# The end of batch 1: where a unit's products and the copies of batch 2's k and q stand

## The chip, the cores and the metric

The kernel runs on one core of one Trainium2 chip. The metric is the device time of one execution in microseconds (us), the median over several runs. A profiled execution gives the trace that the views are taken from. The engines are PE (matrix products; PEld is its loading of weights), DVE (vector), ACT (scalar and activation), POOL (general) and SP (here only a queue that issues DMAs).

## The reference

An attention with a sliding window and a bias by distance, followed by a feed-forward layer with a hard-swish gate:

```
scores = q k^T / sqrt(64) - slope[h] * |i - j|,   kept where 0 <= i - j < 128, else -1e9
attn   = softmax(scores);   x = attn v          # 8 batches, 8 heads, 576 tokens, head size 64
h      = x w_in                                 # 4608 tokens x 512 -> 2048
out    = (h * clip(h + 3, 0, 6) / 6) w_out      # -> 4608 x 512
```

All inputs and the output are float32; the kernel computes its products in bfloat16.

## The kernel before

**Groups.** Attention works on groups of two heads of one batch: `g = 4 * batch + pair`, 32 groups in all; NP is 4. Batch 1 is groups 4 to 7, batch 2 groups 8 to 11. A group's steps are: k and q turned so that the head dimension lies on the partitions (by PE transposes and copies out of PSUM for batches 0 to 2 and k of batch 3, by DMA transposes, line 218, later on); scores (L399 from batch 2 on); exponentials on ACT and cuts by POOL; `attend` or `values`, the products with v (L455, L463) and DVE's division by the row sums (L484, L485); and `back`, which turns the result into `xT`, the input of the feed-forward layer (L517 on PE, the copy L519 on ACT, and on DVE for the last group of batches 0 and 1; by DMA, L510, for most groups from 8 on).

**Units.** The feed-forward layer is cut into token tiles of 512 (`nt`, 9 of them). A tile has 16 up steps (`moe_up`: four 128x512 products over the four pairs of heads, L532; ACT's L556; DVE's L557, which writes `gbuf`) and 16 down steps (`moe_down`, four products L587 each; every fourth ends with a copy and an output DMA). `units` lists them in a fixed order, first the 16 up steps of tile 0 (called unit 0 to 15 here), then up steps of tile 1 (units 16, 17, ...) mixed with down steps of tile 0 by ORDER. `fill(n)` emits the next n of them. `up_begin(nt, ms, n)` emits the first n products of an up step early; the later `fill` completes it. Tile 1 needs all four groups of batch 1 in `xT`, and its fourth product reads the rows of group 7.

**PSUM.** Eight banks: two score tiles of two banks each, used in turn by scores, `attend` and the wide transposes of k and q; "av" and "o" with one buffer each; "h" with two buffers, used in turn. An up step takes a buffer of "h" unless UP_BANKS names another bank for it. A buffer is taken again only when its last reader is done, for an up step DVE's L557. Down steps take "o".

**The order is written by hand.** Each engine runs its instructions in the order of the calls; waits on semaphores are put in for data and buffers. The end of batch 1 is the tail of `second_batch`, lines 773 to 791: attends and backs of groups 4 to 7, the wide transposes of batch 2's first k and q (two pairs of heads in one tile, L301, copies L306), and the last up steps of tile 0. Then follow the first two up steps of tile 1 (the second `fill(2)`), the scores of group 8, and `segment`, which runs groups 8 to 31.

**Loads.** SP's queue issues q, k and v of later batches in order, and also the outputs and the DMA transposes; POOL's queue issues the weights (L176, L190). v of batch 2 starts behind a POOL write at line 768.

Of the kernel before, what the change touches and what calls it, by code (L numbers as in the profile page):

```python
# [18 lines left out]
def kernel(  # L19
# [16 lines left out]
    NP = H // 2  # L36
# [7 lines left out]
    n_ks = d_model // 128  # L44
# [42 lines left out]
    def score_banks():  # L87
        turns[0] += 1
        return score[turns[0] % 2]
# [99 lines left out]
    def load_w_out(g):  # L189
        nc.gpsimd.dma_start(  # L190
            out=w_out_sb[:, ts(g, 4), :],
            in_=moe_w_out[ds(g * 512, 512), :].rearrange("(m p) d -> p m d", p=128))
# [98 lines left out]
    def wide_double(b, dp, nm, copy):  # L291
        wide_begin(b, dp, nm)
        wide_copy(b, dp, nm, 0, 2, copy)

    def wide_begin(b, dp, nm):
        src = st[b, dp, nm]
        wide = score_banks()
        tp = wide.rearrange("p s c -> p (s c)").bitcast(BF16)[:, 0:RT * 128].rearrange(
            "p (t c) -> p t c", t=RT)
        for t in range(RT):  # L300
            nc.tensor.transpose(tp[:, t, :], src[:, t, :], ident)  # L301
        st[b, dp, nm, "wide"] = tp

    def wide_copy(b, dp, nm, i, n, copy):
        dst = (qTb if nm == "q" else kTb)[b % 2][:, ds(2 * dp + i, n), :, :]
        copy(out=dst.rearrange("p i j c -> p i (j c)")[:, :, 0:S].rearrange(  # L306
                 "p i (a t) -> p i a t", t=RT),
             in_=st[b, dp, nm, "wide"].rearrange("p t (a i) -> p i a t", i=2)[:, ds(i, n)])
# [26 lines left out]
    def scores_diag(g):  # L335
        rooms(g)
        b, hp = divmod(g, NP)
        qT, kT = qTb[b % 2][:, hp, :, :], kTb[b % 2][:, hp, :, :]
        first = not diag_tabled(g)
        if (g, "scd") not in st:  # L340
            tables_diag(g)
        scd = st[g, "scd"]
        for j in range(4):
            for e in range(2):
                r = slice(e * D, (e + 1) * D)
                nc.tensor.matmul(scd[:, e, ts(j, 128)], lhsT=kT[r, j, :],
                                 rhs=qT[r, j, :], start=first, stop=first or j == 3)
# [60 lines left out]
    def exp_off_full(g):  # L408
        nc.scalar.activation(out=st[g, "po"].rearrange("p e j c -> p e (j c)"),  # L409
                             in_=st[g, "sco"], func=ACT.Exp, scale=scale)  # L410
# [35 lines left out]
    def av_matmuls(g, qts, where):  # L446
        b, hp = divmod(g, NP)
        vb = vbuf[b % 2]
        pd, po, p4 = st[g, "pd"], st[g, "po"], p4buf[g % 2]
        for qt in qts:  # L450
            for e in range(2):
                h = 2 * hp + e
                out_av = where(qt, e)
                if qt > 0:
                    nc.tensor.matmul(out_av, lhsT=po[:, e, (qt if full(g) else qt - 1) % 4, :],  # L455
                                     rhs=vb[:, qt - 1, h, :], start=True, stop=False)
                if qt < 4:
                    d = pd[:, e, qt, :]
                elif full(g):
                    d = po.rearrange("p e j c -> p e (j c)")[:, e, 64:192]  # L460
                else:
                    d = p4[:, e, :]
                nc.tensor.matmul(out_av, lhsT=d, rhs=vb[:, qt, h, :],  # L463
                                 start=(qt == 0), stop=True)
# [13 lines left out]
    def attend(g):  # L478
        wide = score_banks()
        av = wide[:, :, 0:NQ * W].rearrange("p e (j c) -> p e j c", j=NQ)  # L480
        av_matmuls(g, range(NQ), lambda qt, e: av[:, e, qt, :])
        avs = st[g, "avs"] = small.tile([128, NQ, 2, D], BF16, tag="avs", name="avs")
        rc = small.tile([128, 2, NQ, 1], FP32, tag="rcw", name="rcw")
        nc.vector.reciprocal(rc, av[:, :, :, D:W])  # L484
        nc.vector.tensor_tensor(out=avs.rearrange("p j e d -> p e j d"), in0=av[:, :, :, 0:D],  # L485
                                in1=rc.to_broadcast([128, 2, NQ, D]), op=ALU.mult)
# [16 lines left out]
    def by_xbar(g):  # L503
        return g >= XB and g not in (XB + 2, XB + 3)

    def back(g, tag=None):
        b, hp = divmod(g, NP)
        avs = st[g, "avs"].rearrange("p j e d -> p j (e d)")
        if by_xbar(g):
            nc.sync.dma_start_transpose(  # L510
                out=xT[:, hp, ds(b % 4 * S, SP)].rearrange("p (j c) -> p j c", j=NQ),
                in_=avs.rearrange("p j c -> p (j c)"))
            return
        tag = tag or ("o" if b < 2 else "h")
        tp = BANKS[tag].tile([128, SP], BF16, tag=tag, name="tb", padded_shape=[128, 1024])
        for j in range(NQ):
            nc.tensor.transpose(tp[:, ts(j, 128)], avs[:, j, :], ident)  # L517
        eng = nc.vector.tensor_copy if g in (NP - 1, 2 * NP - 1) else nc.scalar.copy
        eng(out=xT[:, hp, ds(b % 4 * S, S)], in_=tp[:, 0:S])  # L519
# [5 lines left out]
    def up_mms(nt, ms, k0, k1, hps):  # L525
        at0 = nt * NT % RING
        n = min(NT, RING - at0)
        for lo, hi, src in ((0, n, at0), (n, NT, 0)):
            if lo == hi:
                continue  # L530
            for ks in range(k0, k1):
                nc.tensor.matmul(hps[:, lo:hi], lhsT=w_in_sb[:, ks, ts(ms, 128)],  # L532
                                 rhs=xT[:, ks, ds(src, hi - lo)],
                                 start=(ks == 0), stop=(ks == n_ks - 1))

    def up_begin(nt, ms, n, tag="h"):
        hps = BANKS[tag].tile([128, NT], FP32, tag=tag, name="hps")
        up_mms(nt, ms, 0, n, hps)
        begun[nt, ms] = hps, n
# [3 lines left out]
        up_mms(nt, ms, k0, n, hps)  # L543
        begun[nt, ms] = hps, n

    UP_BANKS = {6: "o", 8: "av", 11: "o", 12: "av"}

    def moe_up(nt, ms):
        gts[nt] = gbuf[nt % 2]
        hps, n = begun.pop((nt, ms), (None, 0))  # L550
        if hps is None:
            tag = UP_BANKS.get(ms, "h") if nt == 0 else "h"
            hps = BANKS[tag].tile([128, NT], FP32, tag=tag, name="hps")
# [55 lines left out]
    def fill(n):  # L609
        for _ in range(n):  # L610
            if at[0] == len(units):
                return
            nt, fn, step = units[at[0]]
            if fn is moe_up and done[0] < NP * (min((nt * NT + NT - 1) // S, B - 1) + 1):
                return
            fn(nt if fn is moe_up else nt - 1, step)
            at[0] += 1

    V, P, A = nc.vector.tensor_copy, nc.gpsimd.tensor_copy, nc.scalar.copy
# [109 lines left out]
    def second_batch():  # L729
        scores_diag(NP + 0)  # L730
        exp_diag(NP + 0, 0)
        exp_diag(NP + 0, 1)
        up_begin(0, 2, n_ks, "av")
        scores_off(NP + 0)
        exp_off_full(NP + 0)
        wide_double(1, 1, "k", V)
        fill(2)
        scores_diag(NP + 1)
        exp_diag(NP + 1, 0)
        exp_diag(NP + 1, 1)  # L740
        double(1, 1, "q", 0, "o", V)
        scores_off(NP + 1)
        exp_off_full(NP + 1)
        double(1, 1, "q", 1, "av", V)
        fill(5)
        cast_tokens(1, "v")
        scores_diag(NP + 2)
        exp_diag(NP + 2, 0)
        exp_diag(NP + 2, 1)
        fill(1)  # L750
        scores_off(NP + 2)
        exp_off_full(NP + 2)
        fill(2)
        load_w_out(0)
        load_w_out(1)
        g = 2 * NP - 1
        scores(g)
        exp_diag(g, 0)
        exp_diag(g, 1)
        exp_off_full(g)  # L760
        up_begin(0, 12, n_ks, "av")
        attend(NP)
        fill(1)
        prepare_double(2, 0, (A, P))
        load_w_out(2)
        load_w_out(3)
        prepare_double(2, 1, (P, P))
        nc.gpsimd.memset(ldbuf[2][:, 0:1], 0.0)
        load_tokens(2, "v")
        for dp in range(2):  # L770
            load_double(3, dp, "k", nc.sync)
        load_tokens(3, "q")
        up_begin(0, 13, n_ks)
        attend(NP + 1)
        back(NP, "o")
        attend(NP + 2)
        back(NP + 1, "av")
        attend(NP + 3)
        fill(1)
        back(NP + 2, "o")  # L780
        wide_begin(2, 0, "k")
        wide_copy(2, 0, "k", 0, 2, A)
        up_begin(0, 14, 2)
        back(2 * NP - 1, "av")
        wide_begin(2, 0, "q")
        wide_copy(2, 0, "q", 0, 1, V)
        wide_copy(2, 0, "q", 1, 1, A)
        fill(2)
        done[0] = 2 * NP
        fill(2)  # L790
        scores(2 * NP)
# [98 lines left out]
```

## Time and profile before

| what | value |
|---|---|
| median of 3 runs | 321.89 us (321.74 to 322.06) |
| the profiled execution's own time | 321.99 us |
| its span, first to last instruction | 320.3 us |
| granted PE clock, mean | 0.998 |
| PE busy in 40 to 60 us | 17.55 of 20 us |
| PE busy in 60 to 80 us | 19.82 of 20 us |
| PE busy in 100 to 160 us | 60.00 of 60 us |
| 128x512 product on PE (L532), own duration | 0.38 us; four in a row take 1.03 us |
| L556 on ACT, L557 on DVE | 0.69 us each |

Products overlap on PE, so a row of n lasts less than n times one. A wait is written behind the instruction that waited, with what ended it. An engine's idle time matters only where the end of the run hangs on it.

### The profile page before, as it was taken

Reading aid. Unit: us, or ns where it says so; the run is one execution under the profiler, and the core shown is the slowest. Engines: PE = TensorE matmul, PEld = TensorE weight load, DVE = VectorE, ACT = ScalarE, POOL = GpSimd, SP = SyncE. Lnnn points to the kernel's source line nnn. Section 1 sums busy time; section 2 is a strip of 40 time slices with the busy share of each in tenths; the row PEclk is TensorE's granted clock in tenths of the full one; section 3 lists DMA queues with packets and bytes.
Section 4 is the critical chain, followed back from the end, with each engine's and each line's share of the span. In section 5 each row is a group of like instructions: output and inputs, shape, how many; then the busy total and the mean of one; then the engine's idle time right before and its main releaser. Section 6 shows DMA issues by size and latency. Waiting matters only on the chain.

```text
span 320.3 us, 7022 instructions
## 1 busy us (share of the span) xinstructions
PE 310.0 (97%) x2710; PEld 162.8 (51%) x2710; DVE 175.9 (55%) x344; ACT 197.6 (62%) x339; POOL 138.6 (43%) x247
## 2 busy tenths in 40 slices
PE   7889997999999999999999999999999999999996
PEld 3465463455555444444667654444444444444443
DVE  6677674554445664656455646564656455455510
ACT  3879985777677775767576757675764344244401
POOL 7367290666395685638563855472331000000000
PEclk9999999999999999999999999999999999999999
DMA  7999999889999999999999989925022200100112
GB/s 268 260 371 213 268 239 212 228 208 193 201 255 167 221 226 221 211 221 207 185 177 227 222 183 199 232 60 89 20 55 70 72 33 33 35 33 33 65 53 80
DMA packets 131425, 52.43 MB, mean 164 GB/s; under 512 B 118976, under 2 KB 122816, under 8 KB 131392
## 3 DMA queue, kind: packets, MB, share of 16 engines
q1 hardware_dynamic: 125648, 46.15, 65.7%
q0 software_dynamic: 3696, 3.67, 7.1%
q10 hardware_dynamic: 2048, 2.16, 2.2%
q8 instruction: 21, 0.34, 0.5%
q14 instruction: 12, 0.10, 0.1%
HBM read 36.70 MB, written 9.44 MB: 144 GB/s over the span
## 4 chain that ended last, share of the span: by engine, by line
PE 86%; DMA 5%; ACT 4%; DVE 2%; POOL 1%; issue 1%; SPq 0%; DVEq 0%; POOLq 0%; ACTq 0%
PE ops L587 37%; PE hps L532 37%; PE score L399 3%; DMA ldbuf<-in_q_dram 3%; PE av L463 2%; DMA ldbuf<-in_k_dram 2%; PE av L455 2%; ACT r L556 2%; PE ops L568 1%; DVE gbuf L557 1%; ACT gbuf L425 1%; PE tp L269 1%; PE score L301 1%; ACT gbuf L409 1%; PE tb L517 1%
## 5 line engine op out<-in xcount | busy, mean ns | idle before, releaser
L556 ACT ACTIVATE r<-hps,bias 128x512 f32<-128x512 f32 x144 | 99.0, 689 | 85.3 <-PE hps L532 85.0
L557 DVE SCALAR_TENSOR_TENSOR gbuf<-r,hps 128x512 bf16<-128x512 f32 x144 | 98.7, 687 | 94.3 <-ACT r L556 92.4
L532 PE MATMUL hps<-xT,w_in_sb 128*128 128x512 bf16 (+1 forms) x640 | 143.6, 358 | 2.1 <-DVE gbuf L557 1.8
L587 PE MATMUL ops<-w_out_sb,gbuf 128*128 128x512 bf16 x560 | 138.2, 379 | 0.0
L532 PEld LDWEIGHTS <-w_in_sb 128*128 128x128 bf16 x640 | 59.1, 98 | 55.8 <-issue 3.2
L587 PEld LDWEIGHTS <-gbuf 128*128 128x128 bf16 x560 | 52.4, 98 | 57.5
L427 POOL TENSOR_SCALAR_AFFINE_SELECT pd<-pd 128x512 bf16<-128x512 bf16 x48 | 29.4, 631 | 41.1 <-ACT pd L425 41.1
L436 POOL TENSOR_SCALAR_AFFINE_SELECT po<-po 128x512 bf16<-128x512 bf16 x48 | 30.2, 632 | 32.3 <-ACT po L434 31.6
L596 DVE COPY osb<-ops 128x512 f32<-128x512 f32 x33 | 22.7, 687 | 23.8 <-PE ops L587 23.7
L425 ACT ACTIVATE pd<-score,bias_d 128x512 bf16<-128x512 f32 x48 | 31.1, 684 | 6.4 <-PE score L399 6.4
L434 ACT ACTIVATE po<-score,bias_o 128x512 bf16<-128x512 f32 x48 | 33.1, 690 | 0.0
L213 POOL CAST tbuf<-ldbuf 128x512 bf16<-128x512 f32 (+1 forms) x45 | 25.5, 611 | 12.5 <-issue 12.5
L474 DVE TENSOR_TENSOR avs<-av,rc 128x384 bf16<-128x384 f32 (+1 forms) x48 | 23.6, 491 | 1.6
L463 PEld LDWEIGHTS <-pd 128*128 128x128 bf16 x192 | 14.3, 97 | 8.2 <-POOL tbuf L213 0.2
L455 PE MATMUL av<-vbuf,po 128*128 128x65 bf16 x192 | 18.0, 193 | 0.0
L463 PE MATMUL av<-vbuf,pd 128*128 128x65 bf16 x192 | 17.3, 194 | 0.0
L206 POOL CAST vbuf<-ldbuf 128x1024 bf16<-128x1024 f32 x14 | 14.2, 1041 | 6.0 <-DMA ldbuf<-in_v_dram 6.0
L455 PEld LDWEIGHTS <-po 128*128 128x128 bf16 x192 | 14.3, 98 | 3.0 <-DVE avs L474 0.5
L439 ACT ACTIVATE p4buf<-score,bias_d 128x64 bf16<-128x64 f32 x48 | 15.6, 325 | 0.0
L399 PEld LDWEIGHTS <-kTb 64*64 64x64 bf16 x480 | 9.4, 106 | 9.1 <-issue 8.5
L399 PE MATMUL score<-qTb,kTb 64*64 64x192 bf16 (+1 forms) x480 | 13.1, 234 | 0.0
L246 POOL CAST pr<-ldbuf 128x576 bf16<-128x576 f32 x18 | 11.5, 668 | 2.9 <-ACT w_out_sb L422 1.5
(107 smaller groups left out, 200.7 us busy)
## 6 DMA issues: line engine op xcount, KB each, us to landing
out_dram<-osb SPq DMA_DIRECT2D x33, 256.0 KB, 3.1
ldbuf<-in_v_dram SPq DMA_DIRECT2D x31, 256.0 KB, 4.5
ldbuf<-in_q_dram SPq DMA_DIRECT2D x20, 256.0 KB, 4.6
ldbuf<-in_k_dram SPq DMA_DIRECT2D x16, 256.0 KB, 5.3
ldbuf<-in_q_dram SPq DMA_DIRECT2D x12, 288.0 KB, 6.2
ldbuf<-in_k_dram SPq DMA_DIRECT2D x12, 288.0 KB, 6.1
w_out_sb<-in_moe_w_out_dram POOLq DMA_DIRECT2D x4, 512.0 KB, 9.8
w_in_sb<-in_moe_w_in_dram POOLq DMA_DIRECT2D x3, 512.0 KB, 9.4
```

Of the source, the lines that this page charges most:

```text
L213: nc.gpsimd.tensor_copy(out=tbuf[:m, :, j, :], in_=s[:m, j, :, :].rearrange("p (i e) d -> p i (e d)", e=2))
L399: nc.tensor.matmul(wide[e][c, ds(at, n)], lhsT=kT[r, j, c], rhs=qT[r, ds(q0, n)], start=True, stop=True)
L425: nc.scalar.activation(out=pd[:, e, :, :], in_=block_scores(g, e, False), func=ACT.Exp, bias=bias_d[:, h:h + 1], scale=scale)
L427: nc.gpsimd.affine_select(out=pd[:, e, :, :], in_=pd[:, e, :, :], pattern=[[0, 4], [1, 128]], channel_multiplier=-1, base=0, compare_op=AL ...
L434: nc.scalar.activation(out=po[:, e, :, :], in_=sc, func=ACT.Exp, bias=bias_o[:, h:h + 1], scale=scale)
L436: nc.gpsimd.affine_select(out=po[:, e, :, :], in_=po[:, e, :, :], pattern=[[0, 4], [-1, 128]], channel_multiplier=1, base=-1, compare_op=A ...
L455: nc.tensor.matmul(out_av, lhsT=po[:, e, (qt if full(g) else qt - 1) % 4, :], rhs=vb[:, qt - 1, h, :], start=True, stop=False)
L463: nc.tensor.matmul(out_av, lhsT=d, rhs=vb[:, qt, h, :], start=(qt == 0), stop=True)
L532: nc.tensor.matmul(hps[:, lo:hi], lhsT=w_in_sb[:, ks, ts(ms, 128)], rhs=xT[:, ks, ds(src, hi - lo)], start=(ks == 0), stop=(ks == n_ks - 1))
L556: nc.scalar.activation(out=r6, in_=hps, func=ACT.Relu, bias=bias3[:, 0:1], scale=1.0 / 6.0)
L557: nc.vector.scalar_tensor_tensor(out=gts[nt][:, ms, :], in0=r6, scalar=1.0, in1=hps, op0=ALU.min, op1=ALU.mult)
L587: nc.tensor.matmul(ops[nt, sub], lhsT=gts[nt][:, ms, ts(sub, 128)], rhs=w_out_sb[:, ms, :], start=(ms == 0), stop=(ms == n_ms - 1))
```

## The change

Four things are edited, all around the end of batch 1. Unit 14's products are emitted at once, and ahead of the second back (group 5) rather than in two parts around the last back. The L556 and L557 of units 13 and 14 are emitted together after the last attend, ahead of the copy of group 6's back and of the copies of k and q. The copy of q is one instruction on DVE instead of one half on DVE and one on ACT; k's copy stays one instruction on ACT. Unit 15 takes bank "o" instead of a buffer of "h", so units 16 and 17 take the two "h" buffers that units 13 and 14 held.

```diff
-    UP_BANKS = {6: "o", 8: "av", 11: "o", 12: "av"}
+    UP_BANKS = {6: "o", 8: "av", 11: "o", 12: "av", 15: "o"}
...
         attend(NP + 2)
+        up_begin(0, 14, n_ks)
         back(NP + 1, "av")
         attend(NP + 3)
+        fill(2)
+        back(NP + 2, "o")
+        wide_double(2, 0, "k", A)
+        back(2 * NP - 1, "av")
+        wide_double(2, 0, "q", V)
         fill(1)
-        back(NP + 2, "o")
-        wide_begin(2, 0, "k")
-        wide_copy(2, 0, "k", 0, 2, A)
-        up_begin(0, 14, 2)
-        back(2 * NP - 1, "av")
-        wide_begin(2, 0, "q")
-        wide_copy(2, 0, "q", 0, 1, V)
-        wide_copy(2, 0, "q", 1, 1, A)
-        fill(2)
         done[0] = 2 * NP
         fill(2)
         scores(2 * NP)
```

`wide_double(b, dp, nm, copy)` is `wide_begin` followed by one `wide_copy` of both pairs. Nothing is computed differently.

## The prediction

> **What bounds the kernel now.** The page comes first: its head gives the span of the profiled execution, its first part the busy time of each engine.
>
> ```profile
> span 320.3 us, 7022 instructions
> PE 310.0 (97%) x2710; PEld 162.8 (51%) x2710; DVE 175.9 (55%) x344; ACT 197.6 (62%) x339; POOL 138.6 (43%) x247
> ```
>
> PE is busy for 310.0 of 320.3 us, so a microsecond is to be had only where PE stands still. After the first 28 us, PE's list of waits has two long entries, both in the stretch that the diff edits: 0.58 us ended by DVE's L485 and 1.60 us ended by DVE's L557. From 52 us on there are five waits of 0.08 to 0.18 us and none longer. The table by windows (length, busy time of PE, PEld, DVE, ACT, POOL, granted clock, DMA share, GB/s) shows the place:
>
> ```profile
> 46.00:48.00 2.00, 2.00 (x22) 1.24 (x20) 1.96 (x4) 1.42 (x2) 2.00 (x5) 1.00 1.07 150
> 48.00:50.00 2.00, 0.60 (x3) 0.20 (x2) 0.64 (x2) 1.81 (x3) 0.60 (x2) 1.00 1.23 200
> 50.00:52.00 2.00, 1.79 (x8) 0.68 (x7) 0.75 (x2) 0.69 (x1) 0.00 (x0) 1.00 1.24 204
> ```
>
> PE is idle while ACT is full. The chain of waits (start, length, what) names who is late:
>
> ```profile
> 47.30 1.31 PE hps L532 x6
> ...
> 48.67 0.70 ACT r L556
> ...
> 49.46 0.70 DVE gbuf L557
> ...
> 50.20 1.89 PE hps L532 x8
> ```
>
> The eight products from 50.20 are units 16 and 17. Unit 16 takes the "h" buffer that unit 14 held, which is free only after unit 14's L556 and L557. The timelines of ACT and DVE (start, length, engine and line) say why those came so late:
>
> ```profile
> 46.28 1.14 ACT L306 COPY kTb<-score 128x1152 bf16<-128x1152 bf16 x1
> 48.13 0.64 ACT L306 COPY qTb<-score 128x576 bf16<-128x576 bf16 x1 [0.71 <-DVE qTb L306]
> 48.67 1.27 ACT L556 ACTIVATE r<-hps,bias 128x512 f32<-128x512 f32 x2
> ```
>
> ```profile
> 45.45 0.82 DVE L485 TENSOR_TENSOR avs<-score,rcw 128x640 bf16<-128x640 f32 x1
> 46.19 0.68 DVE L557 SCALAR_TENSOR_TENSOR gbuf<-r,hps 128x512 bf16<-128x512 f32 x1
> 46.84 0.46 DVE L519 COPY xT<-tb 128x576 bf16<-128x576 bf16 x1
> 47.34 0.76 DVE L306 COPY qTb<-score 128x576 bf16<-128x576 bf16 x1
> ```
>
> ACT finishes k's copy at 47.42, stands 0.71 us until DVE has copied the first half of q, copies the second half, and only then turns to unit 14.
>
> **The change, part by part.** On PE, ACT and DVE the order changes; the instructions of POOL and SP stay the same and in the same order, and no DMA is moved. One instruction disappears: q's two copies (DVE 0.76, ACT 0.64) become one DVE copy of 1152 elements. I follow each engine, with 0.216 us per 128x512 product (four from 41.16 to 42.03) and 0.056 us per transpose.
>
> PE. Group 6's attend ends its issue at 43.41. Unit 14's four products now stand there: 4 x 0.216 = 0.86, to 44.28. The second back (group 5) began at 44.15, after the 0.58 us wait, so it starts 0.13 later and the wait is filled. Attend of group 7 moves with it by 0.12. Back of group 6 still starts at 45.14, when its L485 is done (45.08). Its transposes and k's end at 45.93, as now. Unit 14's first two products stood next (0.43 us) and are gone, so PE waits: the last back needs group 7's L485, now 45.57 to 46.39, hence starts at 46.47 (46.36 before). Transposes of the last back and of q take 14 x 0.056 = 0.78, to 47.25. Unit 15: 0.86, to 48.11. Units 16 and 17: 8 x 0.216 = 1.73, to 49.84. Then come the scores of group 8, with the same 0.09 us before them as now: **49.93 instead of 52.02, a gain of 2.09 us**. That is the removed 1.60, plus the 0.58 us hole now used, less the new waits.
>
> Whether everything else is ready by then decides the sum.
> - ACT: copy for group 5 at 44.76; the L556 of units 13 and 14 at 45.30 and 45.87 (0.57 to 0.58 apart, as in every dense row); copy for group 6 at 46.45 to 47.09 (45.76 before); k's copy 46.97 to 48.11; unit 15's L556 48.30 to 48.99; unit 16's 49.16.
> - DVE: L557 of unit 13 at 46.30 to 46.99 and of unit 14 to 47.58; the last back's copy to 47.96; q's copy to 49.3; L557 of unit 15 to about 49.9.
> - So unit 15 finds bank "o" free at 47.1 (needed 47.25). Unit 16 finds unit 13's buffer free at 47.0 (needed 48.11), and for its fourth product, which reads group 7's rows of xT, the copy of 47.96 (needed 48.76). Scores find k at 48.1 and q at 49.3 (needed 49.93). The first down step, which takes bank "o" after unit 15, finds it at 49.9 (needed 50.41).
>
> The tightest of these is unit 15's, 0.15 us. Behind unit 15 on PE stand units 16 and 17 and the scores, and every us that the copy for group 6 is late past 47.1 + 0.15 costs one.
>
> The single q copy has a row. On L306, DVE's longest is 1356 ns, for 1152 elements:
>
> ```profile
> L306 DVE COPY kTb<-score x3: 748/758/1356, 22.2 to 27.6; 128x576 bf16<-128x576 bf16 x2, 128x1152 bf16<-128x1152 bf16 x1
> ```
>
> From both sides: not under one half's 0.76, not over two halves, 1.51. I take 1.36. At 1.51 the scores still have 0.5 us to spare, so it is priced at nothing, covered by units 15 to 17 on PE (2.6 us); without that cover it would cost the scores up to 1.4.
>
> What else must be on time 2.09 us earlier? The weights w_out (L190): by their issues and landings the four groups are there at 47.9, 51.3, 54.3 and 57.5. The four first down steps ran at 52.50, 54.52, 57.62 and 60.51; less 2.09 they need them at 50.4, 52.4, 55.5 and 58.4. Hidden, by 0.9 us at the last. v of batch 2 lands by 61.5 whatever PE does: POOL's casts (L206, L209 from 61.71) want to begin at 59.6, and lose 0.3 us to v and then 0.3 to k of batch 3 (62.56, 63.31). The first products that read v ran at 65.04, wanted 62.95; the v blocks that they read are cast by 61.9. Hidden too.
>
> From 53 to 250 us the rest follows PE, except what follows the loads. SP's queue runs without a break from 48.6 to 88.9 us and again from 105 to 148 (rows end to end, DMA share about 1), so it has a pace of its own. The tightest place is batch 4's k:
>
> ```profile
> 104.95 3.71 SPq L218 DMA_TRANSPOSE kTb<-tbuf  x1
> ```
> ```profile
> DMA to landing us min/median/max: 6.9/6.9/6.9
> ```
> ```profile
> 113.61 0.55 PE L399 MATMUL score<-qTb,kTb 64*64 64x192 bf16 x20
> ```
>
> It lands at 111.85 for scores at 113.61: 1.76 us of room where 2.09 is wanted. But SP stood from 88.89 to 90.78 for an output that DVE copies at 90.07, and that copy comes 2.09 earlier; so k's loads, the transposes and this landing can come up to 1.8 earlier, and the room suffices. The next such places are back of group 15 (lands 123.01, read at 124.82) and of group 19 (154.87, 156.64; here SP stood 2.38 us before).
>
> [...]
>
> Sum: 320.3 - 2.1 = 318.2 us of span. The profiled execution took 321.99, so 1.7 lie outside it, and 319.9 is its new time; it stands 0.1 above the median of the runs shown, 321.89, hence **319.8** for a median.
>
> **The rivals.**
> - Loads at their own pace: landing of batch 4's k stays at 111.85, scores of group 16 start at 111.9 instead of 113.61. Gain 1.7, **320.2**. For it: the unbroken SP queue. Against: SP's 1.83 us pause.
> - The stall only moves: q's copy on DVE, behind two L557 and the last back's copy, becomes what the scores wait for. To halve the gain it must end at 50.9, so take about 3 us; **320.9**. For it: L306 is now one instruction and scores need all of it. Against: the 1356 ns row, and POOL's casts, which end at 48.56, ran beside the half copy of 47.34 (0.76) without stretching it.
> - The change gives nothing: PE gets ahead and the loads of a later batch take it back; about **321.7**. That needs a landing later than today's, for which no row speaks.
> - Slower: k's transpose of batch 4 shares the DMA engines with v4's loads, let go just before it. In this trace k's transposes take 5.5 to 7.6 us, q's 5.1 to 5.3. Released earlier against a backlog of q4 and outputs, they may queue behind more of it. It decides from a landing at 113.6 on (now 111.85); at 114.5 the scores start 0.9 late and the time is **322.8**.
>
> **How the numbers follow.** Chances: forecast 0.68, loads' own pace 0.14, moved stall 0.05, nothing 0.05, slower 0.08. About 0.2% (0.64 us) is what a measurement of this kernel tells from no change. The first three are faster by more than that: 0.87; same 0.05; slower 0.08. Range: at the top 320.9, which takes in the second case and the edge of the third. At the bottom, the three small PE waits at 55.9, 59.65 and 65.69 (0.13, 0.13, 0.18) might close as well: 319.8 - 0.44 = 319.4, rounded out to 319.3.
>
> **What would show it.** Right: unit 14's products at 43.4, no PE wait over 0.6 us between 44 and 52, one of about 0.5 before the last back, scores of group 8 at 49.9; batch 4's k landing about 110 and scores of group 16 at 111.5; the same distance kept to the end. Wrong: a PE wait released by L519 (unit 15), by L306 or by L557 before 50 us; waits before L399 at 111 or before L532 at 122; w_out named before L587.

## The result, and the profile after

| | before | after |
|---|---|---|
| median, runs side by side (17 each) | 322.23 us (321.74 to 323.62) | 320.12 us (319.47 to 322.11) |
| profiled execution: span | 320.3 us | 317.9 us |
| first product of group 4's attend to first score product of group 8, on PE (called D) | 11.41 us | 9.30 us |
| first score product of group 8 to the last product | 265.23 us | 265.22 us |

The ratio is 0.9941, 95% interval 0.9926 to 0.9956: faster by 2.1 us (1.4 to 2.4 by the interval). One run of the changed kernel in a later series took 359.37 us, at a granted clock of 0.852 where all others have 0.995 or more; no ratio uses it. D is read from two lines of PE's timeline (start, length), before

```profile
40.62 0.22 PE L463 MATMUL score<-vbuf,gbuf 128*128 128x65 bf16 x2
52.02 0.55 PE L399 MATMUL score<-qTb,kTb 64*64 64x192 bf16 x20
```

and after:

```profile
40.36 0.23 PE L463 MATMUL score<-vbuf,gbuf 128*128 128x65 bf16 x2
49.66 0.55 PE L399 MATMUL score<-qTb,kTb 64*64 64x192 bf16 x20
```

In the two profiled executions the spans differ by 2.35 us. D carries 2.11 of it; group 4's attend, ahead of everything that was edited, starts at 40.36 instead of 40.62, which is the rest and differs from one execution to the next. From group 8 on nothing was given back in this execution.

The page's head and first part of the kernel after:

```profile
span 317.9 us, 6980 instructions
PE 307.0 (97%) x2671; PEld 163.4 (51%) x2710; DVE 176.1 (55%) x344; ACT 196.8 (62%) x338; POOL 138.9 (44%) x247
```

The records of 39 products are missing from this trace (2671 of 2710 are there), so PE's busy times are not to be compared; the work is the same. The table by windows, the same stretches as before:

```profile
46.00:48.00 2.00, 1.76 (x18) 1.28 (x20) 2.00 (x5) 1.85 (x3) 2.00 (x4) 1.00 1.06 144
48.00:50.00 2.00, 2.00 (x27) 0.92 (x26) 1.85 (x3) 1.61 (x3) 1.16 (x3) 1.00 1.18 193
50.00:52.00 2.00, 2.00 (x27) 0.97 (x16) 1.07 (x2) 0.46 (x1) 0.00 (x0) 1.00 1.23 204
```

PE, at 0.60 of 2 us between 48 and 50 before, is now full there. The chain of waits no longer passes through ACT's L556 and DVE's L557 at this place; it stays on PE from the last back to the scores:

```profile
45.30 0.83 DVE avs L485
46.14 0.05 issue
46.19 0.45 PE tb L517 x5
46.64 0.50 PE score L301 x9
47.14 0.21 PE hps L532
47.36 0.05 issue
47.41 2.32 PE hps L532 x10
49.73 0.48 PE score L399 x18
```

PE's list of waits between 43 and 60 us has one entry left (what waited, what ended it; total, times, longest), the new wait before the last back:

```profile
PE tb L517 <- DVE avs L485: 0.3, 1, 0.3
```

The timelines of ACT and DVE after:

```profile
45.03 1.27 ACT L556 ACTIVATE r<-hps,bias 128x512 f32<-128x512 f32 x2
46.18 0.65 ACT L519 COPY xT<-tb 128x576 bf16<-128x576 bf16 x1
46.70 1.15 ACT L306 COPY kTb<-score 128x1152 bf16<-128x1152 bf16 x1
48.04 0.69 ACT L556 ACTIVATE r<-hps,bias 128x512 f32<-128x512 f32 x1 [0.19 <-PE hps L532]
```

```profile
46.04 1.27 DVE L557 SCALAR_TENSOR_TENSOR gbuf<-r,hps 128x512 bf16<-128x512 f32 x2
47.24 0.45 DVE L519 COPY xT<-tb 128x576 bf16<-128x576 bf16 x1
47.60 1.35 DVE L306 COPY qTb<-score 128x1152 bf16<-128x1152 bf16 x1
48.87 1.51 DVE L557 SCALAR_TENSOR_TENSOR gbuf<-r,hps 128x512 bf16<-128x512 f32 x2
```

Units 13 and 14 stand side by side on both engines, ahead of the copies, and are done at 47.3 instead of 50.2. Unit 14 no longer waits for k and q to be copied.

### The profile page after: what moved, and what is told of

Same layout as the page of the kernel before. It is cut to its first block, busy times and chain, and to the rows that moved or that the text cites. A ratio compares the mean times of both kernels' runs of the same rounds, so it can differ in the third digit from the quotient of the medians.

```text
span 317.9 us, 6980 instructions
## 1 busy us (share of the span) xinstructions
PE 307.0 (97%) x2671; PEld 163.4 (51%) x2710; DVE 176.1 (55%) x344; ACT 196.8 (62%) x338; POOL 138.9 (44%) x247
## 4 chain that ended last, share of the span: by engine, by line
PE 90%; ACT 3%; DVE 3%; issue 2%; POOL 0%; DVEq 0%; POOLq 0%; ACTq 0%
PE hps L532 38%; PE ops L587 37%; PE score L399 3%; PE av L463 2%; PE av L455 2%; DVE avs L485 1%; PE ops L568 1%; PE w L163 1%; ACT w_out_sb L422 1%; PE score L346 1%; PE tp L269 1%; ACT r L556 1%; DVE gbuf L557 1%; PE score L301 1%; PE score L357 1%
## 5 line engine op out<-in xcount | busy, mean ns | idle before, releaser
L556 ACT ACTIVATE r<-hps,bias 128x512 f32<-128x512 f32 x144 | 98.9, 689 | 84.2 <-PE hps L532 83.9
L557 DVE SCALAR_TENSOR_TENSOR gbuf<-r,hps 128x512 bf16<-128x512 f32 x144 | 98.8, 688 | 91.6 <-ACT r L556 90.1
L532 PE MATMUL hps<-xT,w_in_sb 128*128 128x512 bf16 (+1 forms) x623 | 142.0, 358 | 1.7 <-ACT xT L519 0.3
L587 PE MATMUL ops<-w_out_sb,gbuf 128*128 128x512 bf16 x538 | 133.8, 379 | 2.3 <-issue 1.8
L532 PEld LDWEIGHTS <-w_in_sb 128*128 128x128 bf16 x640 | 59.2, 98 | 54.0 <-issue 1.5
L427 POOL TENSOR_SCALAR_AFFINE_SELECT pd<-pd 128x512 bf16<-128x512 bf16 x48 | 29.4, 631 | 35.2 <-ACT pd L425 35.2
L436 POOL TENSOR_SCALAR_AFFINE_SELECT po<-po 128x512 bf16<-128x512 bf16 x48 | 30.1, 633 | 30.8 <-ACT po L434 30.1
L213 POOL CAST tbuf<-ldbuf 128x512 bf16<-128x512 f32 (+1 forms) x45 | 25.7, 611 | 15.7 <-issue 14.6
```

Of the source, the lines that this page charges most:

```text
L213: nc.gpsimd.tensor_copy(out=tbuf[:m, :, j, :], in_=s[:m, j, :, :].rearrange("p (i e) d -> p i (e d)", e=2))
L427: nc.gpsimd.affine_select(out=pd[:, e, :, :], in_=pd[:, e, :, :], pattern=[[0, 4], [1, 128]], channel_multiplier=-1, base=0, compare_op=AL ...
L436: nc.gpsimd.affine_select(out=po[:, e, :, :], in_=po[:, e, :, :], pattern=[[0, 4], [-1, 128]], channel_multiplier=1, base=-1, compare_op=A ...
L556: nc.scalar.activation(out=r6, in_=hps, func=ACT.Relu, bias=bias3[:, 0:1], scale=1.0 / 6.0)
L557: nc.vector.scalar_tensor_tensor(out=gts[nt][:, ms, :], in0=r6, scalar=1.0, in1=hps, op0=ALU.min, op1=ALU.mult)
L587: nc.tensor.matmul(ops[nt, sub], lhsT=gts[nt][:, ms, ts(sub, 128)], rhs=w_out_sb[:, ms, :], start=(ms == 0), stop=(ms == n_ms - 1))
```

## The experiments

D is read from one profile of each kernel. It repeats to 0.01 us (9.30, 9.30 and 9.29 in three profiles of the changed kernel), while medians of whole runs differ by some tenths between series of runs. A ratio given with a run is against the kernel before in the same series.

**The bank alone.** Unit 15 takes bank "o", and nothing else is changed:

```diff
-    UP_BANKS = {6: "o", 8: "av", 11: "o", 12: "av"}
+    UP_BANKS = {6: "o", 8: "av", 11: "o", 12: "av", 15: "o"}
```

> The kernel before with one edit: unit 15 takes bank o. D is the time on PE from the first product of group 4's attend to the first score product of group 8: 11.41 us before, 9.30 after the change. Theory (the stall has two causes, the late L556 and L557 of unit 14 and too few free h buffers): unit 16 no longer waits, unit 17 then waits for unit 14's L557 until the same moment at which unit 16 waited, so 4 x 0.216 = 0.86 is gained, D = 10.55, with a PE wait of about 0.9 left. Rival (the bank alone removes the stall): D = 9.8 or less, no wait.

D is 10.55. PE's list of waits of this kernel, from 43 to 110 us:

```profile
PE hps L532 <- DVE gbuf L557: 0.9, 2, 0.7
PE tb L517 <- DVE avs L485: 0.6, 1, 0.6
PE av L455 <- POOL po L436: 0.4, 1, 0.4
```

Unit 17 now waits where unit 16 did (0.74 of the first line). The expected 0.86 is there in D, but the runs show less: 0.9987 (0.9972 to 1.0001), which is 0.4 us with an interval that takes in no change at all. The last line gives one reason, at 108.0 us: a mask of POOL came late for the products with v, and in this profile 0.53 us were lost between the scores of groups 15 and 16. That place returns below.

**Everything but the bank.**

```diff
-    UP_BANKS = {6: "o", 8: "av", 11: "o", 12: "av", 15: "o"}
+    UP_BANKS = {6: "o", 8: "av", 11: "o", 12: "av"}
```

> The changed kernel with unit 15 back in an h buffer. Theory: unit 15 takes unit 13's buffer, so unit 17 must wait for unit 15's L557, which ended at about 49.55 in the changed kernel, where unit 17 would start at 48.7: a PE wait of about 0.9, D = 10.2. Rival (the order of the L556 and L557 alone is what counts): D = 9.30.

D is 10.18, 0.88 worse than the changed kernel; the runs give 0.9962 (0.9947 to 0.9976) against before. Its waits on PE between 43 and 60:

```profile
PE hps L532 <- DVE gbuf L557: 0.7, 1, 0.7
PE tb L517 <- DVE avs L485: 0.3, 1, 0.3
```

So the three other edits together are worth 11.41 - 10.18 = 1.23 and the bank 0.88 on top of them; alone the bank gives 0.86. Unit 17's wait speaks against the rival: the order of the L556 and L557 is not enough by itself.

**q's copy again in halves.**

```diff
-        wide_double(2, 0, "q", V)
+        wide_begin(2, 0, "q")
+        wide_copy(2, 0, "q", 0, 1, V)
+        wide_copy(2, 0, "q", 1, 1, A)
```

> The changed kernel with q's copy again in two halves, the first on DVE, the second on ACT. Theory: the wait of ACT for DVE's half now only delays unit 15, whose L557 ends at about 50.3 instead of 49.55; the scores are not late (D = 9.30), the first down step is by 0 to 0.3 us. Rival (the split copy with its wait across two engines was the cause of the stall): D = 10.0 or more.

D is 9.30 and the first down step starts 0.25 later against the attend (10.03 for 9.78). ACT's timeline and PE's wait show the detour that remains:

```profile
48.53 0.64 ACT L306 COPY qTb<-score 128x576 bf16<-128x576 bf16 x1 [0.53 <-DVE qTb L306]
49.07 1.27 ACT L556 ACTIVATE r<-hps,bias 128x512 f32<-128x512 f32 x2
```
```profile
PE ops L587 <- DVE gbuf L557: 0.2, 1, 0.2
```

ACT stands 0.53 us for DVE's half as it did before, but only unit 15 is behind it. The single copy is worth a quarter of a microsecond here, not the gain. Runs: 0.9955 (0.9938 to 0.9971) against before.

**The single q copy alone, in the kernel before.**

```diff
-        wide_copy(2, 0, "q", 0, 1, V)
-        wide_copy(2, 0, "q", 1, 1, A)
+        wide_copy(2, 0, "q", 0, 2, V)
```

> The kernel before with one edit: q's copy is one instruction on DVE. Theory: unit 14's L556 no longer waits for the second half, starts at 47.8, but its L557 stands behind the whole q copy on DVE and ends at about 49.35; unit 16 starts about 0.8 earlier than 50.20, D = 10.6. Rival (the split copy is the whole cause): the PE wait of 1.6 is gone, D = 9.8.

D is 10.87, a gain of 0.54 where 0.8 was expected. A mask of group 7 (POOL's L427) was late here: PE waited for it at 44.76, and group 7's L485 starts 5.16 us after group 4's attend instead of 4.83. The 0.33 passes on to q's copy and to unit 14's L557, and covers the 0.27 that is missing. The mechanism is the expected one, by DVE's timeline:

```profile
47.62 1.36 DVE L306 COPY qTb<-score 128x1152 bf16<-128x1152 bf16 x1
48.90 1.42 DVE L557 SCALAR_TENSOR_TENSOR gbuf<-r,hps 128x512 bf16<-128x512 f32 x2
```

Unit 14's L557 stands behind the whole copy and PE still waits 0.76 us for it. Another 0.19 us were lost between the scores of groups 15 and 16, at the place seen with the bank alone. Runs: 0.9979 (0.9970 to 0.9989).

**Unit 14's products behind the last attend.**

```diff
-        up_begin(0, 14, n_ks)
         back(NP + 1, "av")
         attend(NP + 3)
+        up_begin(0, 14, n_ks)
```

> The changed kernel with unit 14's four products behind the last attend instead of ahead of the second back. D as in the other runs: 9.30 in the changed kernel. Theory (the early place fills a PE wait, but DVE's divisions set the pace there): the wait of 0.58 before the second back comes back, the one before the last back goes, D = 9.30 + 0.18 = 9.48. Rival (the early place is what brings unit 14's L556 and L557 forward, and so the gain): D over 10.

D is 9.49. The early place of the products, the first thing that the diff shows, is worth 0.19 us; runs 0.9924 (0.9902 to 0.9946) against before, and not told apart from the changed kernel in the same series (0.9937, 0.9912 to 0.9963). PE's one wait between 43 and 60 is the old one again:

```profile
PE tb L517 <- DVE avs L485: 0.6, 1, 0.6
```

**The changed kernel again, beside the last one.**

> The changed kernel as it is, once more beside the others. Theory: D = 9.3 again, and the time from the first score product of group 8 to the last product is 265.2 us as in the kernel before; where whole runs differ by more, the difference lies ahead of 40 us. Rival (0.25 us of the gain belong to the change too): group 4's attend starts 0.25 us earlier than before again.

D is 9.30, and group 4's attend starts at 41.03, later than before: the 0.25 us do not belong to the change. But from group 8 to the end it took 266.07. PE's timeline of this execution has the reason:

```profile
123.97 1.24 PE L532 MATMUL hps<-xT,w_in_sb 128*128 128x512 bf16 x5 [0.68 <-DMA xT<-avs]
```

The DMA transpose of group 15 (L510) landed at 123.93, 4.8 us after its issue, where it took 3.3 in the first profile of this kernel; 0.85 us were lost. The two times to landing, in this execution and in the first profile:

```profile
DMA to landing us min/median/max: 4.8/4.8/4.8
```
```profile
DMA to landing us min/median/max: 3.3/3.3/3.3
```

So a DMA transpose took back part of the gain in one of three profiled executions.

**Two more loads.** They show how much room the loads have left. In `stage_next`, ahead of the transpose of batch 4's q, into a new tile `spare`:

```diff
+            if g == 12:
+                for j in range(2):
+                    nc.sync.dma_start(out=spare[:, j, :].rearrange("p (h d) -> p h d", h=8),
+                                      in_=q[0, :, ds(j * 128, 128), :].rearrange("h p d -> p h d"))
             cast_tokens(nb, "qk"[hp])
             xbar(nb, "qk"[hp])
```

> The changed kernel with two more loads of 256 KB each on SP's queue, into a buffer that nothing reads, between the loads of batch 4's k and the DMA transpose of its q. Theory (SP's queue has a pace of its own, and batch 4's k has 1.0 us of room left: it lands at 110.24, the scores of group 16 start at 111.24): the landing moves by about 2.4 us, the scores wait about 1.4 and the run is about 1.4 us longer than the changed kernel. Rival (the loads are hidden well enough): no PE wait, no loss.

D is 9.29; from the scores of group 15 to those of group 16 it took 10.17 instead of 8.03, so 2.14 us are lost, and the median is 322.03 where the changed kernel in the same series has 320.54. Six of the ten runs lie between 321.87 and 322.07, the profiled one among them, and four between 323.95 and 325.67; what the four lost is not known. The size was under-estimated, and the way is another one. Batch 4's k landed at 112.39, ahead of its scores at 113.60, and PE did not wait for it. POOL's and PE's timelines (line numbers are one higher in this kernel, L214 is L213):

```profile
102.66 2.83 POOL L214 CAST tbuf<-ldbuf 128x512 bf16<-128x512 f32 x5 [6.38 <-issue]
105.45 1.21 POOL L428 TENSOR_SCALAR_AFFINE_SELECT pd<-pd 128x512 bf16<-128x512 bf16 x2
106.62 1.21 POOL L437 TENSOR_SCALAR_AFFINE_SELECT po<-po 128x512 bf16<-128x512 bf16 x2
```
```profile
106.14 0.20 PE L464 MATMUL av<-vbuf,pd 128*128 128x65 bf16 x1 [0.33 <-POOL pd L428]
107.90 0.20 PE L456 MATMUL av<-vbuf,po 128*128 128x65 bf16 x1 [0.35 <-POOL po L437]
```

POOL stands 6.38 us before casting batch 4's k, because the one `tbuf` is still being read by the DMA transpose of q, which landed at 102.55. The profile names no releaser for this wait, but the cast starts 0.11 us after that landing here, and 0.12 us after it in the changed kernel (100.09 after 99.97). The masks of group 14 are behind that cast in POOL's order, and PE's products with v need them. Without the masks the scores would have been due at about 111.45 (an estimate: 61.58 us after those of group 8, as in the changed kernel), so k's landing would have cost some 0.9; the masks cost more and hid it.

**The same loads in the kernel before.**

> The kernel before with the same two loads of 256 KB ahead of the DMA transpose of batch 4's q. They cost the changed kernel 2.15 us between the scores of groups 15 and 16 (from 7.81 to 10.17 less 0.21 of a later start). Theory (from 89 us on the loads followed PE by 2.0 of its 2.36 us, so the change has used up 0.35 us of room): PE loses about 1.8 us here. Rival (the loads kept their own pace and did not follow): no loss here, since PE is 2.36 us later. Other rival (they followed in full): 2.15 us.

The distance from group 15 to 16 is 10.24 for 8.03, a loss of 2.21: as much as in the changed kernel (the 7.81 in the expectation should read 8.03). The waits of PE are for the same masks:

```profile
PE av L464 <- POOL pd L428: 0.8, 2, 0.4
PE av L456 <- POOL po L437: 0.7, 2, 0.4
```

The runs give 1.0050 (1.0031 to 1.0069), a loss of 1.6 us. The theory's 1.8 was wrong for this profile and the second rival holds in it. q's transpose landed 2.74 us later than in the changed kernel with these loads, and the scores of group 8 started 2.68 later: in these two executions the loads followed PE in full.

**A second tbuf, with the two loads.**

```diff
-    tbuf = held.tile([128, NP, NQ, 128], BF16, name="tbuf")
+    tbufs = {n: held.tile([128, NP, NQ, 128], BF16, name="tbuf" + n) for n in "qk"}
```

and `tbufs[nm]` in `cast_tokens` and `xbar`.

> The changed kernel with the two more loads, and with a tbuf of its own for k, so that POOL's casts of batch 4's k (L213) need not wait for the DMA transpose of its q. Theory (the two loads hurt by way of POOL: its casts wait for tbuf, and the masks of group 14, L427 and L436, stand behind them while PE waits for those): the PE waits ended by L427 and L436 are gone, the loss shrinks from 2.15 to under 0.4 us. Rival (the landing of batch 4's k is what PE waits for): a PE wait before L399 at group 16 and a loss over 1 us.

POOL's wait and all PE waits for masks are gone, and group 15 to 16 takes 8.03 again, as theory said. But the loss did not shrink to 0.4: it moved on to the unit that reads group 15's transpose, where 1.63 us were lost:

```profile
125.63 1.24 PE L533 MATMUL hps<-xT,w_in_sb 128*128 128x512 bf16 x5 [1.47 <-DMA xT<-avs]
```

That transpose landed at 125.59, 4.5 us after its issue, where it took 3.5 with the same loads and one `tbuf`. As an estimate, 1.0 of the 1.63 belongs to this one landing and 0.6 to the loads. The runs, 0.9998 (0.9981 to 1.0016), show no gain left. So there are two limits close behind each other, the masks behind `tbuf` and group 15's transpose; the landing of k is behind both, but close (112.45 for scores at 112.79).

**The second tbuf without the loads, and the changed kernel beside it.**

> The changed kernel with a tbuf of its own for k, without more loads. Theory: in an execution in which no load is late PE has nothing to gain, 265.2 us from the first score product of group 8 to the last product as before; POOL's wait of about 4 us before L213 goes, and the time is that of the changed kernel within 0.3 us or less, as late loads become rarer. Rival (the wait on POOL costs PE time in each execution): 0.5 us or more gained against the changed kernel of the same call.

> The changed kernel as it is, beside the one with two tbufs. Theory: D = 9.3 again; from the first score product of group 8 to the last product 265.2 us, or up to 0.9 more where the DMA transpose of group 15 lands late, as in the second profile. Rival (that loss was a single accident of one execution): 265.2 us.

Both took 265.23 from group 8 to the end. The medians are 321.02 (319.85 to 322.01) and 320.26 (319.97 to 321.43); against before, 0.9957 (0.9938 to 0.9976) and 0.9943 (0.9925 to 0.9960). A second `tbuf` gains nothing where nothing is late, and that it makes late landings rarer is not shown. No version is shown to beat the changed kernel.

## Why the prediction was right, point by point

The forecast was 319.8 and the median is 320.12; the gain of 2.09 that the sum gave is 2.11 in D and 2.11 between the medians. That the medians agree to 0.02 is luck, since their interval is 1.4 to 2.4. The 0.3 by which the time is off comes with the medians: the kernel before stood at 322.23 in the longer series, 321.89 in the runs shown.

- **What bounds it.** Right: the removed wait was the gain. The edits other than the bank carry 1.23 of it and the bank 0.88, and neither removes the stall without the other (D of 10.18, 10.55 and 9.30). With the bank in place, leaving out the early products costs 0.19 and leaving out the single copy nothing in D. That the order of the L556 and L557 gives the rest of the 1.23, about 1 us, is by difference; no run moves it alone.
- **PE's sum.** Right in its parts. Its last sentence does not add up: 1.60 and 0.58 less a new wait of 0.5 make 1.7. The listed waits are short, because they begin at a product's modelled end (a 128x512 product has a record of 0.38 us, and the next is issued 0.216 us after it): counted from the last issue, the two holes were 1.76 and 0.74 us, and another of 0.13 before the back of group 6 went too, which with 0.54 of new wait gives the 2.09. The last back started 5.83 us after group 4's attend where the sum had 46.47 - 40.62 = 5.85; the wait before it, 0.5 us without issue in the sum, is listed as 0.34 because a product still counts as busy until its modelled end (a transpose of k has a record of 0.22 us, the next is issued 0.056 us after it). Moving unit 14's products up is worth 0.19 (expected 0.18).
- **Readiness.** Right: units 15 to 17 and the scores waited for nothing. Unit 15, the tightest, found its bank free: its first product starts at 46.98, right behind q's transposes (46.48 plus 9 x 0.056). The chain's short stretch called issue at 47.36 stands where a product's record is missing.
- **The single copy.** Right on the row: q's copy took 1.35 us against 1.36 from L306:

```profile
L306 DVE COPY qTb<-score x2: 758/1053/1348, 24.2 to 47.6; 128x576 bf16<-128x576 bf16 x1, 128x1152 bf16<-128x1152 bf16 x1
```

  In this row 576 elements took 0.76 us, so the one copy came out 0.17 under two halves.
- **w_out and v.** Right: PE did not wait for w_out or for batch 2's v.
- **Batch 4's k.** Its own numbers came true, seen in SP's timeline, in the time to landing and in PE's timeline:

```profile
102.94 3.69 SPq L218 DMA_TRANSPOSE kTb<-tbuf  x1
```
```profile
DMA to landing us min/median/max: 7.3/7.3/7.3
```
```profile
111.24 0.55 PE L399 MATMUL score<-qTb,kTb 64*64 64x192 bf16 x20
```

  It landed at 110.24 ("about 110") with 1.0 us of room. But the step "The tightest place is batch 4's k" was wrong. It looked only at transfers that PE itself waits for and passed over POOL, which waits for the same transposes with masks queued behind. The trace before has the sign of it in POOL's timeline, 0.11 us after q's transpose landed at 101.98:

```profile
102.09 2.83 POOL L213 CAST tbuf<-ldbuf 128x512 bf16<-128x512 f32 x5 [3.66 <-issue]
```

  The second L436 mask of group 14 ends 0.65 us ahead of the product that reads it in the kernel before, and only 0.29, 0.16 and 0.15 ahead in the three profiles of the changed kernel, where k keeps 1.0 to 1.6. So the forecast held past a limit that it had not looked at, and by little: that is luck. With the bank alone and with the single copy alone, 0.53 and 0.19 us were lost there without any more loads. By the runs the masks of group 14 come first, group 15's transpose next, and k's landing was never the bound.
- **The rivals.** "Loads at their own pace" gave 1.7 us of gain. In one of three profiles of the changed kernel a late DMA transpose did take 0.85 back, at the place of group 15 that the prediction named as the next, and the wait before L532 that it listed as a sign of being wrong was there. In the other two it took nothing. How far the loads follow PE differs: batch 4's k landed 1.61 us earlier after the change while its scores came 2.37 earlier, and with two more loads they followed in full. The moved stall, nothing and slower did not come; the halves of q's copy showed that the scores did not depend on it.

What stays open: how often group 15's transpose lands late, and why it took 4.8 us once. Over the thirteen profiled executions of all kernels here it took 3.0 to 3.6 us in eleven, and 4.5 and 4.8 in two. The spread of the changed kernel's runs (319.47 to 322.11) is not shown to come from it.

## What to carry to other kernels

Where two units wait for buffers, ask first which instruction frees the buffer and what stands ahead of it on its engine; a free bank alone saved the products of one unit (0.86 us) and handed the wait to the next, until that order was changed too. The most visible line of a diff may be the least of it: of 2.11 us the early products gave 0.19, and the bank with the order behind them nearly all. When PE gets ahead of a queue of loads, look for the next limit also on the engines that wait for those loads with other work queued behind, not only at the instruction that reads the data.

## What the runs showed of the hardware

The same DMA transpose, at the same place of SP's queue, landed 3.3 us after its issue in one execution of the changed kernel and 4.8 in another. Two loads of 256 KB ahead of a DMA transpose moved its landing by 2.4 us (102.55 for 99.97, less 0.21 of a later start), although SP issued them in 1.92; this is one execution of each kernel.
